# One change in five parts to a fused attention and feed-forward layer: shared score tenancies in PSUM, reversed denominator order, a first projection in halves, interleaved memory features, and an input loaded straight into the residual buffer

## The chip, the cores and the metric

The kernel runs on one core of a Trainium2 chip. Times are device microseconds of whole executions; a median is over the runs named beside it. The profile of an execution gives its span, which is 1.7 to 2.0 us shorter than its time (914.6 for 916.63). Kernels are compared only within the same rounds.

## The reference, cut to what matters

2048 tokens of width 1024, 32 heads of 32, four segments of 512 tokens. Each segment has causal attention inside itself and reads a memory `M`, `z` that the earlier segments have filled. Then come a projection, a residual and a gated feed-forward part of width 3584.

```python
h = x + _A_ref(_layernorm(x), A_wq, A_wk, A_wv, A_wo, A_beta)
h2 = h + _B_ref(_layernorm(h), B_w1, B_w3, B_w2)
# in _A_ref, for each segment s of 4:
p = _softmax(q @ k * scale + mask);  a_dot = p @ v
pq = phi(q);  a_mem = (pq @ M) / (pq @ z + 1e-6)      # phi(t) = t + 1 if t > 0, else exp(t)
outs.append(g * a_mem + (1 - g) * a_dot)
pk = phi(k);  M = M + pk @ v;  z = z + sum(pk)
```

## The kernel before

The kernel describes all its work as operations with a cost, a class (a lower number goes first) and the buffers that they read and write. Before anything runs, a scheduler plays the operations through with rough costs and fixes the order of each engine's instructions. The chip keeps that order (all 5472 weight loads of TensorE come in the same order in the changed kernel's trace and in e1's): if an operation takes longer than its estimate, what stands behind it on its engine waits (in e10 an exponential stands on ScalarE behind a feature exponential that waited 1.37 us). This is the part of it that the argument needs:

```python
# schedule(), cut: an operation on an engine is taken by class, when its inputs are ready
if o.patience and mode == "full" and now < o.offered + o.patience:
    skipped.append(item)          # a column block waits a while rather than change the array's use
    ...
if not can_start(o):              # no free PSUM bank
    skipped.append(item)
```

The kernel divides PSUM, the memory that TensorE writes into, into eight banks. A tenancy is one stay of results in banks, from the first matmul that writes them to the read that frees them. Banks 0 to 3 are for one score tenancy at a time, 4 and 5 hold the values and denominators of a head group, and 6 and 7 serve all dense work (projections, memory updates, output projection):

```python
def dense_group(self, late=False):
    g = Group([(6,), (7,)], ("att", [(4,), (5,), (0,), (1,), (2,), (3,)]) if late else None, True)
```

A head group is four heads, and its attention is a "unit". TensorE uses the array in three ways: full (128x128), rows (four scores at once on 32 rows each), and columns (four value or denominator matmuls at once on 32 columns each). In the timelines these are `128*128`, `32*128` and `128*32`, and the four of a set start within 0.012 us.

```python
def unit(self, s, g, q, k, v, pq):                     # cut
    for batch in (0, 1, 2):
        gr = self.queue(0, 1, 2, 3)
        kcs = ((0,), (1,), (2, 3))[batch]
        width = (512, 384, 384)[batch]                  # three tenancies per unit
        ...                                             # 4 or 8 score matmuls, then one exp
    for kc, src in pieces():                            # values and denominators alternate
        for g_, what in ((gn, "n"), (gd, "d")):
            ...
    # o1 = values * ocol * R0;  o2 = Nm * R1;  oT = o1 + o2

def wo_stage(self, s):                                  # cut
    for i in range(4):
        t = 4 * s + i
        xr, h, hn = self.xr[0], self.h[t % 2], self.hn[0]
        self.g.dma(xr[:, :], self.x2d[t * 128:(t + 1) * 128, :], cls=2)
        for half in range(2):
            gr = self.dense_group(s >= 2)
            ...                                         # 8 matmuls with wo
            # h = xr + PSUM on VectorE, class 3, which frees the dense bank
        self.ln(16 + t, h[:, :], hn[:, :], 4)           # statistics, then hn from h
```

The softmax here doesn't subtract the row's maximum and nothing guards it: scores larger than these inputs give would overflow.

## Time and profile before

| | before |
|---|---|
| time, median of 3 | 918.27 us (917.35 to 918.42) |
| span of the profiled execution | 914.6 us |
| streaming of all matmul columns | 874.3 us |
| changes of array use | 234, at 0.109 us: 25.5 us |
| head: waits and clock ramp up to the first projection | 6.8 us |
| waits of TensorE after it | 3.65 us |
| end: drain and store after the last matmul | 2.9 us |

How to read it: the streaming is every matmul's columns / 2.4 GHz + 2.5 ns, a set of four row-tiled or column-tiled matmuls counted once. This is the line through the spacings in the trace of before: the next matmul, or set, of the same use starts after 0.0557 us at 128 columns, 0.1092 at 256, 0.1625 at 384 and 0.2158 at 512. A change of use is counted at 0.109 us; the prediction lists the measured medians, 0.104 to 0.116. The clock ramp is in the starts of the first matmuls of 512 columns: about 0.43 us apart up to 4.2 us, 0.216 from 4.5 us on. The head is the time from TensorE's first instruction (1.24 us) to the first projection, less the streaming between. The waits are what remains between the first projection and the last matmul. The prediction shows the lines of the page, the timeline of the array's changes, and the head.

### The profile page before, as it was taken

The numbers are of one execution on the slowest core, as the hardware profiler recorded it, in microseconds if no ns is written. First come the engines' busy times: TensorE is split into PE (matmuls) and PEld (weight loads), VectorE is DVE, ScalarE is ACT, GpSimd is POOL, SyncE is SP. The second block draws the span as 40 slices with busy tenths as digits, with TensorE's granted clock in tenths as the row PEclk, the third lists the DMA queues.
The fourth block names the chain that finished last, engine by engine and source line by source line (L and its number), as shares of the span: only waits on it lengthen the run. The fifth ranks groups of instructions, "written<-read, shape, count | busy, mean of one in ns | idle before, by whom it ended". The sixth has DMA issues, their size and how long they took to land.

```text
span 914.6 us, 12864 instructions
## 1 busy us (share of the span) xinstructions
PE 895.2 (98%) x5346; PEld 402.7 (44%) x5440; DVE 431.8 (47%) x739; ACT 295.2 (32%) x330; POOL 173.5 (19%) x274
## 2 busy tenths in 40 slices
PE   7999999999999999999999999999999999999998
PEld 3444444444444444444444444444444444444443
DVE  3677857788767775644634411211343334431111
ACT  4777546886777751111111100000111111110000
POOL 3454505665554441100100000000000000000000
PEclk9999999999999999999999999999999999999999
DMA  9769774542513119543733121012133212301110
GB/s 310 196 186 220 163 203 125 152 120 94 137 47 93 47 51 319 144 131 93 205 94 93 51 65 47 21 34 83 48 98 92 67 48 70 93 24 41 35 40 29
DMA packets 145241, 96.26 MB, mean 105 GB/s; under 512 B 45344, under 2 KB 132384, under 8 KB 145184
## 3 DMA queue, kind: packets, MB, share of 16 engines
q1 hardware_dynamic: 145184, 95.45, 37.9%
q8 instruction: 43, 0.70, 0.3%
q14 instruction: 14, 0.11, 0.0%
HBM read 76.55 MB, written 8.39 MB: 93 GB/s over the span
## 4 chain that ended last, share of the span: by engine, by line
PE 95%; DVE 2%; issue 1%; ACT 1%; DMA 0%; POOL 0%; SPq 0%; ACTq 0%
PE ps L604 88%; PE ps L927 4%; PE ps L874 3%; DMA xs<-in_A_x_dram 0%; DVE lnst L725 0%; DVE h L982 0%; DVE t L1011 0%; DVE hm L1016 0%; ACT eA L889 0%; ACT sg L1008 0%; PE ps L616 0%; ACT eB L889 0%; DVE T L938 0%; ACT xnT L627 0%; DVE xs L734 0%
## 5 line engine op out<-in xcount | busy, mean ns | idle before, releaser
L604 PE MATMUL ps<-hnT,w1b 128*128 128x512 bf16 x877 | 220.6, 379 | 1.4 <-issue 0.6
L604 PE MATMUL ps<-hnT,w3b 128*128 128x512 bf16 x877 | 220.2, 379 | 1.3 <-issue 0.5
L1008 ACT ACTIVATE sg<-ps 128x512 bf16<-128x512 f32 x112 | 66.9, 597 | 427.7 <-PE ps L604 427.7
L604 PE MATMUL ps<-w2b,hm 128*128 128x512 bf16 x878 | 195.4, 379 | 0.9
L1011 DVE SCALAR_TENSOR_TENSOR t<-sg,ps 128x512 bf16<-128x512 bf16 x112 | 76.9, 687 | 195.3 <-ACT sg L1008 195.1
L604 PEld LDWEIGHTS ps<-w2b,hm 128*128 128x128 bf16 x896 | 87.6, 98 | 105.8
L604 PEld LDWEIGHTS ps<-hnT,w3b 128*128 128x128 bf16 x896 | 87.0, 98 | 104.8 <-issue 0.9
L604 PEld LDWEIGHTS ps<-hnT,w1b 128*128 128x128 bf16 x896 | 87.0, 98 | 104.4 <-issue 5.5
L1016 DVE SCALAR_TENSOR_TENSOR hm<-t,ps 128x512 bf16<-128x512 bf16 x112 | 76.9, 687 | 37.3 <-PE ps L604 34.1
L1038 DVE TENSOR_TENSOR ob<-hr,ps 128x512 bf16<-128x512 bf16 x32 | 22.0, 687 | 143.4 <-PE ps L604 143.4
L889 ACT ACTIVATE eA<-ps 128x2048 bf16<-128x2048 f32 x32 | 60.0, 1875 | 15.2 <-PE ps L874 11.1
L604 PE MATMUL ps<-xnT,wp 128*128 128x512 bf16 x246 | 59.4, 380 | 3.7 <-issue 1.3
L604 PE MATMUL ps<-hnT,wp 128*128 128x512 bf16 x248 | 59.4, 380 | 1.5 <-issue 0.8
L604 PE MATMUL ps<-wo,oT 128*128 128x512 bf16 x247 | 58.3, 379 | 1.1 <-issue 0.6
L889 ACT ACTIVATE eB<-ps 128x1536 bf16<-128x1536 f32 x32 | 46.3, 1448 | 12.7 <-PE ps L874 12.6
L889 ACT ACTIVATE eC<-ps 128x1536 bf16<-128x1536 f32 x32 | 46.4, 1450 | 10.4 <-PE ps L874 10.4
L894 POOL TENSOR_SCALAR_AFFINE_SELECT eC<-eC 128x512 bf16<-128x512 bf16 x64 | 41.2, 667 | 44.0 <-ACT eC L889 44.0
L938 DVE STREAM_TRANSPOSE T<-ps 128x512 f32<-128x512 f32 x32 | 22.9, 716 | 31.5 <-PE ps L927 31.3
L604 PEld LDWEIGHTS ps<-wo,oT 128*128 128x128 bf16 x256 | 23.9, 98 | 28.9 <-issue 2.1
L604 PEld LDWEIGHTS ps<-xnT,wp 128*128 128x128 bf16 x256 | 22.9, 98 | 30.4 <-issue 3.9
L604 PEld LDWEIGHTS ps<-hnT,wp 128*128 128x128 bf16 x256 | 23.4, 98 | 28.9 <-issue 2.6
L874 PE MATMUL ps<-qT,kT 32*128 32x256 bf16 (+3 forms) x512 | 34.5, 302 | 0.4 <-ACT eB L889 0.3
(98 smaller groups left out, 718.0 us busy)
## 6 DMA issues: line engine op xcount, KB each, us to landing
w1b<-in_B_w_dram SPq DMA_DIRECT2D x28, 512.0 KB, 3.9
w3b<-in_B_w_dram SPq DMA_DIRECT2D x28, 512.0 KB, 4.9
wp<-in_A_wk_dram SPq DMA_DIRECT2D x8, 1024.0 KB, 5.8
wp<-in_A_wv_dram SPq DMA_DIRECT2D x8, 1024.0 KB, 6.1
wp<-in_A_wq_dram SPq DMA_DIRECT2D x7, 1024.0 KB, 6.4
w2b<-in_B_w_dram SPq DMA_DIRECT2D x7, 1024.0 KB, 8.1
xs<-in_A_x_dram SPq DMA_DIRECT2D x16, 256.0 KB, 6.9
xr<-in_A_x_dram SPq DMA_DIRECT2D x16, 256.0 KB, 3.1
```

Of the source, the lines that this page charges most:

```text
L604: return [e.matmul(p[0](gr), p[1], p[2], start=p[3], stop=p[4]) for p in part]
L874: ins.append(e.matmul(self.bank(gr, j, n, off), k[r, g, 128 * kc:128 * kc + 128], q[r, g, 128 * kc:512], start=True, stop=True, tile_posit ...
L889: return [e.activation(et[:, :, :], src, AF.Exp, scale=self.scale)]
L894: self.pool_op(lambda e, m=m: e.affine_select(m, m, pattern=[[0, 4], [1, 128]], compare_op=ALU.is_ge, fill=0.0, base=0, channel_multiplier ...
L927: ins.append(e.matmul(self.ps[r, b * 512 + 128 * kc:(b + 1) * 512], lhsT, src[:, j, :], start=first, stop=True, tile_position=(0, 32 * j), ...
L938: G.op("dve", dve_ns(512), lambda e, gr: [e.transpose(T1, self.bank(gr))], writes=[T1], cls=0, group=gd)
L1008: self.g.op("act", act_ns(512), lambda e, gr, sg=sg: [e.activation(sg, self.bank(gr), AF.Tanh, scale=0.5)], writes=[sg], cls=2, group=gg)
L1011: e.scalar_tensor_tensor(t1, sg, 1.0, self.bank(gr), op0=ALU.add, op1=ALU.mult)], reads=[sg], writes=[t1], cls=2,
L1016: e.scalar_tensor_tensor(dst, t1, 0.5, self.bank(gr), op0=ALU.mult, op1=ALU.mult)], reads=[t1], writes=[dst], cls=2,
L1038: self.g.op("dve", dve_ns(512), lambda e, gr, hs=hs, ob=ob: [e.tensor_tensor(ob, hs, self.bank(gr), op=ALU.add)], reads=[hs], writes=[ob], ...
```

## The change

The intent: fewer changes of array use, a shorter start, and dense work spread more evenly through attention. Five parts, with the diff cut to its core:

```diff
 # (1) two head groups share five full tenancies (6 shared score buffers), not six of 512, 384, 384;
 #     to make room, the sums of a unit are made in place
+        ta = self.scores(s, [(a, 0, 0)])
+        tb = self.scores(s, [(a, 3, 384), (a, 1, 0)])
+        tc = self.scores(s, [(a, 2, 0), (b, 2, 256)])
+        self.finish(s, a, ...)
+        ta = self.scores(s, [(b, 0, 0)])
+        tb = self.scores(s, [(b, 3, 384), (b, 1, 0)])
+        self.finish(s, b, ...)
...
-        dst = o1 if s else oT
+        dst = R0 if s else oT
...
-            self.either(lambda e: e.tensor_tensor(o2, Nm, R1, op=ALU.mult), ...
-            self.either(lambda e: e.tensor_tensor(oT, o1, o2, op=ALU.add), ...
+            self.either(lambda e: e.tensor_tensor(Nm, Nm, R1, op=ALU.mult), ...
+            self.either(lambda e: e.tensor_tensor(oT, R0, Nm, op=ALU.add), ...
 # (2) denominators in reverse order, and column blocks may wait longer for a turn
+            order = [("n", 0), ("n", 1), ("n", 2), ("n", 3), ("d", 3), ("d", 2), ("d", 1),
+                     ("d", 0)]
-        o.patience = 2600.0
+        o.patience = 4000.0
 # (3) the first query projection by token halves
+                if n == 0:
+                    self.first_q(w)
+                    continue
 # (4) key features and memory updates interleaved (query features already were); residual and memory
 #     additions in class 1
+            if s:
+                self.phi(self.qT[s % 2][:, 2 * pr:2 * pr + 2, :], self.pq[pr % 2][:, :, :], 3)
+            if s < 3:
+                self.memory(s, pr)
+            self.pair(s, pr)
...
-                self.memory(s)
 # (5) x goes straight into the residual buffer, of which there are three; the staging buffer goes
-            xr, h, hn = self.xr[0], self.h[t % 2], self.hn[0]
-            self.g.dma(xr[:, :], self.x2d[t * 128:(t + 1) * 128, :], cls=2)
+            h, hn = self.h[t % 3], self.hn[0]
+            self.g.dma(h[:, :], self.x2d[t * 128:(t + 1) * 128, :], cls=2)
...
-                    hs, xs, self.bank(gr), op=ALU.add)], reads=[xs], writes=[hs], cls=3,
+                    hs, hs, self.bank(gr), op=ALU.add)], reads=[hs], writes=[hs], cls=1,
```

The prediction treats (4) and (5) together, as its part 4. The whole diff also puts the other projections in class 5 instead of 6, changes two of the scheduler's cost estimates (scores and column blocks) and drops an unused mask.

## The prediction

One passage is cut from the prediction; its mark stands where it was. The sum came to 918.3 - 3.05 - 1.8 + 0.1 - 0.6 = 912.95 us. The -0.6 is the author's estimate; the rest is worked out from the trace of before and the edit, and that trace has 50 matmuls of the feed-forward part starting in 10.79 us (0.2158 each) and about 0.11 us for a change of use. That the weight loads run under the matmuls is on its page: 402.7 us of loads beside 895.2 of matmuls in a span of 914.6.

> **What bounds the kernel now.** I read the page first: busy shares, the granted clock, the chain that ended last.
>
> ```profile
> PE 895.2 (98%) x5346; PEld 402.7 (44%) x5440; DVE 431.8 (47%) x739; ACT 295.2 (32%) x330; POOL 173.5 (19%) x274
> PEclk9999999999999999999999999999999999999999
> PE 95%; DVE 2%; issue 1%; ACT 1%; DMA 0%; POOL 0%; SPq 0%; ACTq 0%
> ```
>
> TensorE is busy 98% and its own instructions are 95% of the chain that ended last, at full granted clock; no other engine reaches half of the span. So a saving on VectorE, ScalarE, GpSimd or the DMA queues is worth only the TensorE wait that it removes. The sharper question is what lies between TensorE's 914.6 us and the bare streaming of its columns. For that I read the timeline of TensorE, matmul by matmul, in the attention part.
>
> ```profile
> 200.44 0.28 PE L927 MATMUL ps<-eC,v 128*32 128x256 bf16 x4
> 200.55 0.28 PE L927 MATMUL ps<-eC,ones 128*32 128x256 bf16 x4
> 200.66 0.23 PE L927 MATMUL ps<-eC,v 128*32 128x128 bf16 x4
> 200.72 0.23 PE L927 MATMUL ps<-eC,ones 128*32 128x128 bf16 x4
> 201.11 0.81 PE L604 MATMUL ps<-xnT,wp 128*128 128x512 bf16 x3 [0.16 <-issue]
> 201.85 0.40 PE L874 MATMUL ps<-qT,kT 32*128 32x512 bf16 x4
> 202.18 0.63 PE L604 MATMUL ps<-v,pkn 128*128 128x129 bf16 x8
> ```
>
> The first column is the start, and starts are what to subtract; the second is a latency that overlaps. Four row-tiled or column-tiled matmuls start within 0.01 us and share the array, so a set of four 256-column ones takes 0.11 us, of 128 columns 0.06 us. A set of 512 columns should take 0.216 us, but from the scores at 201.85 to the next full matmul 202.18 - 201.85 = 0.33 us pass: 0.11 us too many. I computed this excess at every boundary between the three uses of the array (full 128x128, row-tiled scores, column-tiled value and denominator matmuls), against columns/2.4 GHz plus 2.5 ns per matmul. The medians: full to row 0.106, row to full 0.111, row to column 0.109, full to column 0.104 us, whatever the width that stands last.
>
> Column to full looks dearer (201.11 - 200.72 = 0.39, an excess of 0.34), but it is a trap. There are 5440 weight loads and 5346 matmuls, so 94 matmul records are missing; here the timeline has three of the group's four, and two weight loads before the first recorded one (0.876 and 0.891 past 200). The missing matmul therefore started near 200.89, and the excess is 0.34 - 0.22 = 0.12 us like the others. Two such boundaries with complete records show 0.116 us.
>
> The budget of the 914.6 us then is: streaming of all 5440 matmuls 874.3; 234 changes of array use at 0.109, 25.5; start before the first real projection about 8 (clock ramp and waits, 1.2 us before the first instruction); waits inside the attention part 3.1, the longest 0.67, 0.59 and 0.50; the rest is the final drain and store. The streaming is out of the change's reach.
>
> The head comes from the timeline of the first 26 us:
>
> ```profile
> 4.73 1.67 PE L604 MATMUL ps<-oT 128*128 128x512 bf16 x7
> 9.01 1.61 PE L616 MATMUL ps<-ident,xs 128*128 128x128 bf16 x24 [2.60 <-DVE xs L734]
> 11.49 0.61 PE L616 MATMUL ps<-ident,xs 128*128 128x128 bf16 x8 [0.87 <-DVE xs L734]
> 13.30 10.60 PE L604 MATMUL ps<-xnT,wp 128*128 128x512 bf16 x47 [1.21 <-ACT xnT L627]
> ...
> 9.66 2.01 ACT L627 ACTIVATE xnT<-ps 128x1024 bf16<-128x1024 bf16 x2 [2.74 <-PE ps L616]
> 10.19 0.69 DVE L628 COPY xnT<-ps 128x1024 bf16<-128x1024 bf16 x1
> 12.13 1.02 ACT L627 ACTIVATE xnT<-ps 128x1024 bf16<-128x1024 bf16 x1 [0.46 <-PE ps L616]
> ```
>
> The first projection waits for all four token tiles; the last is copied out of PSUM only at 12.13 + 1.02 = 13.15, though tiles 0 and 1 are there at about 10.7 and 10.9.
>
> [...] the largest gap here is 2.6 us and the granted clock stays full, so shortening the head buys only its own time.
>
> **The change part by part.**
>
> 1. Scores in full tenancies. Before, a head group has three PSUM tenancies of 512, 384 and 384 columns, 96 in all; after, two groups share five of 512, 80 in all. Columns are the same (2 x 1280 = 5 x 512), so streaming is not reduced. What goes is visits: 16 fewer row-tiled blocks. With the scheduler's reordering, the built program's TensorE order has 235 blocks of like use before (107 full, 96 row, 32 column) and 207 after (95, 80, 32): 28 changes fewer. 28 x 0.109 = 3.05 us, all on the path since TensorE is it. On ScalarE, 2048-element exponentials take 1.875 us and 1536-element ones 1.449, so a fixed part of about 0.17 us (estimate by the line through both): 64 x 1.449 + 32 x 1.875 = 152.7 becomes 80 x 1.875 = 150.0. These 2.7 us are beside the path.
>
> 2. Reverse order of the denominator. It puts the 512-column set last in 24 of 32 column blocks. If the apparent 0.34 us were real this would save 23 x 0.23 = 5.3 us. By the missing record above it isn't, so I book 0. Equal weights follow each other, but each is loaded again and the loads already run under the matmuls.
>
> 3. First query by token halves. By the new order: tiles 0 to 2 transposed, then the first 8 half matmuls, tile 3 transposed, then the rest. Start at about 11.0 (copies done at 10.9; the second half of the weights lands at 10.3); 8 x 0.109 = 0.87 to 11.87; eight transposes at 0.056 to 12.32, copied out by about 13.5; 24 x 0.109 = 2.62 to 14.94, past that copy, so no wait; 32 x 0.109 = 3.49 to 18.4. Before: 13.30 + 32 x 0.216 = 20.2. Gain 1.8 us. The split adds 32 matmuls, 32 x 2.5 ns = 0.08 us.
>
> 4. Interleaved query and key features, memory updates and residual additions at a higher class, x loaded straight into a triple-buffered h. These touch the 3.1 us of waits only:
>
> ```profile
> 219.51 1.04 PE L604 MATMUL ps<-xnT,wp 128*128 128x512 bf16 x4 [0.49 <-DVE h L982]
> 241.32 1.04 PE L604 MATMUL ps<-xnT,wp 128*128 128x512 bf16 x4 [0.18 <-DVE h L982]
> 52.28 1.04 PE L604 MATMUL ps<-xnT,wp 128*128 128x512 bf16 x4 [0.33 <-DVE kT L628]
> 78.23 1.02 PE L604 MATMUL ps<-hnT,wp 128*128 128x512 bf16 x4 [0.42 <-DVE qT L628]
> ```
>
> The first two (excess 0.67 and 0.34) are residual additions late in VectorE's queue, which the higher class can cure. The others come from a short 8 x 0.056 = 0.45 us memory group between two dense groups with two banks, shorter than the 0.69 us copy that must free a bank; the new order still has such places. New waits will appear too. I book -0.6 of 3.1.
>
> Sum: 918.3 - 3.05 - 1.8 + 0.1 - 0.6 = 912.95, say 913.0 us, 0.6% faster.
>
> **The rivals.** (a) The apparent column-to-full cost is real: then 5.3 us more go, about 908. For: 30 of those boundaries show 0.34. Against: the extra weight load, and the complete records at 0.116. (b) A new wait takes the place of the visits. In-place R0 and Nm now stay occupied until the final addition, and the shared score buffer lives through both groups of a pair; column blocks wait up to 4.0 us for a turn rather than 2.6. For: all order is fixed at build time from rough costs. Against: a unit lasts some 10 us (320 us for 32), much over these chains of about 1 us each, and dense work stands between. If the waits double, 916 to 917. (c) The head gains nothing, as the next key projection then waits for its weights or for query evictions: weights land at 13.3, well before 18.4, and four evictions at 0.60 run while the last half streams. At worst 914.8. (d) ScalarE becomes the bound: it has 62.9 of 87 us busy from 24 to 111 and loses work, so no.
>
> **Range and chances.** The counts (28 changes) are certain and their price stable to 5%; the head is good to 0.7 us; the waits can move from -2 to +3. Executions spread about 1 us. That gives 910.0 to 916.0. Over 2% faster means under 899.9: without any wait, streaming 874.4, 206 changes 22.5, a head of 6.2, an end of 3.2 and the 3.6 us by which the timed median exceeds the profiled span still make 910, so 1%. Over 2% slower needs 18 us of new waits, six times those of before: 1%.
>
> **What would show it.** Right: 206 changes with the same 0.11 us each; weight loads and matmuls up by 32; first projection at about 11.0 and its end near 18.4; 80 exponentials of about 1.875 us; column to full with 512 last no cheaper than 0.11 to 0.12 us. Wrong: waits in the attention part that sum to more than 4 us, above all of memory groups or score tenancies, or a first key group that starts later than 19.

## More of the kernel before

One more line belongs here, for later. It is a row of the list of instruction groups, ScalarE, of the kernel before:

```profile
L889 ACT ACTIVATE eA<-ps 128x2048 bf16<-128x2048 f32 x32 | 60.0, 1875 | 15.2 <-PE ps L874 11.1 <-PE ps L927 3.8
```

After the bar stand busy time and nanoseconds of one, then ScalarE's idle time just before them and what ended it. The exponential mostly waits for its own scores (11.1 us), and for 3.8 us its wait ends with a column block, which reads the exponentials' buffers.

## The result, and the profile after

The changed kernel took 917.41 us (median of 4, 916.1 to 918.23), the kernel before beside it 918.35 (median of 4, 917.35 to 919.37). The ratio is 0.9988, 95% interval 0.9971 to 1.0006. A ratio here is the mean time of one kernel's fast runs over that of the other's of the same rounds, so it is not quite the ratio of the medians. The time lay 4.4 us above the predicted 913.0 and above the range. Of the 5 us of gain less than 1 was left.

The page of the changed kernel, with the lines that answer to those of the prediction:

```profile
PE 904.0 (99%) x5472; PEld 404.1 (44%) x5472; DVE 432.8 (47%) x735; ACT 297.7 (32%) x316; POOL 176.2 (19%) x274
PEclk9999998999999999999999999999999999999999
PE 96%; ACT 1%; DVE 1%; DMA 0%; issue 0%; SPq 0%; DVEq 0%
```

TensorE is the bound as before. The row of granted clock has an 8 in its seventh slice, where there were only nines. The weight loads and matmuls are both 5472, so no record is missing in this profile.

| budget, profiled execution | before | changed | difference |
|---|---|---|---|
| changes of array use x 0.109 us | 234: 25.5 | 206: 22.45 | -3.05 |
| head | 6.82 | 4.71 | -2.11 |
| waits after it, half clock included | 3.65 | 10.30 | +6.65 |
| span | 914.6 | 916.2 | +1.6 |

The three differences add up to +1.5, which is the span's +1.6 but for 0.1 of streaming. The parts that save did save, and the waits took it back. Next is TensorE's timeline at the start of the changed kernel:

```profile
10.74 1.03 PE L598 MATMUL ps<-xnT,wp 128*128 128x256 bf16 x8 [0.26 <-DVE xnT L622]
11.61 0.61 PE L610 MATMUL ps<-ident,xs 128*128 128x128 bf16 x8
12.06 9.73 PE L598 MATMUL ps<-xnT,wp 128*128 128x256 bf16 x72
21.72 0.40 PE L871 MATMUL ps<-qT,kT 32*128 32x512 bf16 x4
```

The first eight half matmuls start at 10.74 (before 13.30), the fourth tile is transposed right behind them, and the 72 that follow run without a wait. 56 of them are query halves, so the first query ends at 12.06 + 56 x 0.109 = 18.16; the prediction had 11.0 and 18.4.

The disputed change from column to full can be read at the end of a column block, in the changed kernel and in a second profile of the same program (run e1), which has lost 95 of its matmul records:

```profile
89.59 0.23 PE L939 MATMUL ps<-et,ones 128*32 128x128 bf16 x4
89.75 1.90 PE L598 MATMUL ps<-wp,hnT 128*128 128x512 bf16 x8
```

```profile
PE 895.4 (98%) x5377; PEld 404.2 (44%) x5472; DVE 432.7 (47%) x735; ACT 297.7 (32%) x316; POOL 176.1 (19%) x274
...
89.94 0.23 PE L939 MATMUL ps<-et,ones 128*32 128x128 bf16 x4
90.32 1.67 PE L598 MATMUL ps<-wp,hnT 128*128 128x512 bf16 x7 [0.16 <-issue]
```

With all records the next full matmul starts 0.16 us later. With one lost, 7 are listed instead of 8, the gap looks like 0.38 us, and an "issue" wait of 0.16 us appears that does not exist. Over all 30 such boundaries the excess, with the 0.01 us by which the first matmul after a change is longer, is 0.116 us in the complete profile, for 128 columns last (7 cases) and for 512 last (23); in the incomplete one its median is 0.342 for both.

Where did the waits come from? The list of TensorE's waits, first of the kernel before (two of its rows, which the change touches), then of the changed one. The columns are total, times and longest, in us:

```profile
PE ps L604 <- DVE h L982: 0.7, 2, 0.5
PE ps L874 <- ACT eB L889: 0.3, 1, 0.3
```

```profile
PE ps L871 <- ACT et L884: 2.0, 5, 0.8
PE ps L598 <- DVE R0b L970: 1.5, 1, 1.5
PE ps L598 <- DVE h L993: 0.9, 3, 0.6
```

Scores wait for exponentials, and single groups wait for VectorE. Most of it stands in one place, around 150 us. This is the changed kernel's timeline there, cut to what matters:

```profile
144.59 0.83 DVE L725 TENSOR_SCALAR hn<-h,lnmv,rstd 128x1024 bf16<-128x1024 bf16 x1
145.45 1.24 SPq L210 DMA_TRANSPOSE hnT<-hn  x1
146.24 0.71 PE L939 MATMUL ps<-et,ones 128*32 128x128 bf16 x16
146.74 0.58 SPq L203 DMA_DIRECT2D h<-in_A_x_dram  x1
146.89 1.04 PE L598 MATMUL ps<-wo,oT 128*128 128x512 bf16 x4
147.01 1.88 ACT L884 ACTIVATE et<-ps 128x2048 bf16<-128x2048 f32 x1 [1.99 <-PE ps L939]
147.79 0.39 PE L598 MATMUL ps<-pq,zsel 128*128 128x512 bf16 x1
148.94 0.40 PE L871 MATMUL ps<-qT,kT 32*128 32x256 bf16 x8 [0.77 <-ACT et L884]
150.05 0.71 DVE L970 SCALAR_TENSOR_TENSOR R0b<-ps,ocol,R0b 128x512 f32<-128x512 f32 x1
150.68 1.08 DVE L725 TENSOR_SCALAR hn<-h,lnmv,rstd 128x1024 bf16<-128x1024 bf16 x1
150.81 0.52 PE L598 MATMUL ps<-pq,Mbf 128*128 128x512 bf16 x1 [1.47 <-DVE R0b L970]
151.32 0.61 PE L871 MATMUL ps<-qT,kT 32*128 32x512 bf16 x4
151.68 1.27 DVE L993 TENSOR_TENSOR h<-h,ps 128x512 bf16<-128x512 bf16 x2
152.50 1.86 PE L598 MATMUL ps<-hnT,wp 128*128 128x512 bf16 x4 [0.56 <-DVE h L993]
```

Between the last output projection at 146.89 and the next dense group at 152.50 TensorE has no dense work. By the kernel's assignment of banks the two dense ones hold the two finished halves of that projection until the residual additions at 151.68 read them. These additions need x in their residual buffer. Its load was only issued at 146.74: the buffer was read by the layer normalisation of the tile three before until 145.42 (144.59 + 0.83), and a transpose stands ahead of the load in the queue until 146.69. It landed at 150.79, when VectorE had just begun the next normalisation, 150.68 to 151.76. Meanwhile only attention work is left, and it runs bare into its own chains: scores for an exponential of 1.88 us, the memory matmul for VectorE to empty its bank. The waits here are 0.83 + 1.52 + 0.19 + 0.62 = 3.2 us against the pure pitch.

Then the clock falls. The view by stretches of the changed kernel, whose last three columns are granted clock, DMA share and GB/s:

```profile
140.00:147.50 7.50, 7.35 (x72) 3.07 (x69) 6.32 (x13) 4.82 (x4) 5.30 (x8) 1.00 0.55 79
147.50:151.00 3.50, 1.26 (x12) 0.31 (x10) 3.43 (x8) 3.00 (x2) 2.01 (x3) 0.99 0.71 183
151.00:158.00 7.00, 6.44 (x25) 2.58 (x24) 4.10 (x8) 1.55 (x3) 5.30 (x9) 0.52 0.58 132
```

TensorE is busy 1.26 of 3.5 us, and for the next 7 us the granted clock is 0.52: exactly, half clock from 150.95 for 6.83 us, which costs 3.0 us. Other runs show single stretches of 3.41 us (e4, e8, e10). The waits in the hole are no longer than 1.5 us, while at 8.71 us in this same profile TensorE had waited 2.42 us at full clock, and the clock stayed full.

The recorded stretches of full and half clock all begin on a grid of 3.413 us, whose place differs from execution to execution (first mark at 4.17 us in this profile, 4.41 in e1, 6.37 in e4). A window is here the stretch between two marks. The last one before the fall was this:

```profile
147.53:150.94 3.41, 1.17 (x12) 0.31 (x10) 3.34 (x8) 2.91 (x2) 1.95 (x3) 1.00 0.70 182
```

Streaming, by the formula of the budget, fills 0.23 of it. The profiles have six falls inside a program, and the window just before holds 0.23 (here and in e1), 0.24 (e6), 0.27 (e8), 0.29 (e4) and 0.31 (e10). No other window at full clock, in the 17 profiles that record the clock, that ends before the last matmul holds less than 0.36. So in these profiles the fall goes with what is streamed in one window, and not with the longest wait; what makes it is not shown. The same head fell in one profile and not in another: its lowest window holds 0.39 in the profile of the kernel before, at full clock, and 0.29 in that of e4, whose grid lies elsewhere, before the fall.

The fall is not certain. Six executions of the changed kernel in e1 have a mean granted clock of 1.0 (915.72 us), 0.998 (916.21 and 916.63) and 0.996 (917.6 to 918.23). The kernel before has such stretches too: beside e1 to e4 its executions at 1.0 took 916.15 to 917.7, those at 0.998 took 917.9 to 919.1.

So without the half clock the waits are where the prediction's rival b put them: doubled, from 3.65 to about 7.3 us. Why they doubled is what the experiments are for.

### The profile page after: what moved, and what is told of

Same layout as the page of the kernel before. It is cut to its first block, busy times and chain, and to the rows that moved or that the text cites. A ratio compares the mean times of both kernels' runs of the same rounds, so it can differ in the third digit from the quotient of the medians.

```text
span 916.2 us, 12998 instructions
## 1 busy us (share of the span) xinstructions
PE 904.0 (99%) x5472; PEld 404.1 (44%) x5472; DVE 432.8 (47%) x735; ACT 297.7 (32%) x316; POOL 176.2 (19%) x274
## 4 chain that ended last, share of the span: by engine, by line
PE 96%; ACT 1%; DVE 1%; DMA 0%; issue 0%; SPq 0%; DVEq 0%
PE ps L598 89%; PE ps L939 4%; PE ps L871 3%; ACT et L884 1%; DMA xs<-in_A_x_dram 0%; DVE lnst L716 0%; PE ps L610 0%; DVE h L993 0%; DVE hn L725 0%; SPq L203 0%; DVE T L950 0%; DVE R0b L965 0%; DVE R0b L970 0%; DVE qT L622 0%; DVE xnT L622 0%
## 5 line engine op out<-in xcount | busy, mean ns | idle before, releaser
L598 PE MATMUL ps<-hnT,w1b 128*128 128x512 bf16 x896 | 223.2, 379 | 0.0
L884 ACT ACTIVATE et<-ps 128x2048 bf16<-128x2048 f32 x80 | 149.9, 1874 | 34.2 <-PE ps L871 17.9
L889 POOL TENSOR_SCALAR_AFFINE_SELECT et<-et 128x512 bf16<-128x512 bf16 x128 | 88.7, 710 | 118.6 <-ACT et L884 118.3
L598 PE MATMUL ps<-hnT,wp 128*128 128x512 bf16 x256 | 63.5, 390 | 0.9 <-DVE h L993 0.6
L598 PE MATMUL ps<-xnT,wp 128*128 128x512 bf16 (+1 forms) x288 | 60.2, 356 | 0.3 <-DVE xnT L622 0.3
L598 PEld LDWEIGHTS ps<-xnT,wp 128*128 128x128 bf16 x288 | 26.5, 98 | 27.1 <-issue 4.2
L976 POOL TENSOR_TENSOR Nm<-Nm,R1b 128x512 f32<-128x512 f32 x24 | 30.4, 1268 | 32.6 <-DVE R1b L965 32.5
L871 PE MATMUL ps<-qT,kT 32*128 32x128 bf16 (+3 forms) x512 | 31.9, 302 | 2.2 <-ACT et L884 2.0
L598 PE MATMUL ps<-wp,hnT 128*128 128x512 bf16 x128 | 30.8, 380 | 0.0
```

The costliest lines, as they stand in the source:

```text
L598: return [e.matmul(p[0](gr), p[1], p[2], start=p[3], stop=p[4]) for p in part]
L871: ins.append(e.matmul(self.bank(gr, j, 512 - 128 * kc, off), k[r, g, 128 * kc:128 * kc + 128], q[r, g, 128 * kc:512], start=True, stop=Tru ...
L884: return [e.activation(et[:, :, :], src, AF.Exp, scale=self.scale)]
L889: self.pool_op(lambda e, m=m: e.affine_select(m, m, pattern=[[0, 4], [1, 128]], compare_op=ALU.is_ge, fill=0.0, base=0, channel_multiplier ...
L976: self.either(lambda e: e.tensor_tensor(Nm, Nm, R1, op=ALU.mult), 512, 2, [Nm, R1], [Nm], 2)
```

## The experiments

Theory at the start: part (5) makes the hole, because x arrives late in a buffer that is still in use. Rivals: the shared tenancies and buffers do it by themselves; the in-place sums do it; the order of the denominators or the head gives nothing. All runs gave correct results. All differ from the kernel before by less than 2%. Ratios are against the kernel before of the same rounds, times are medians. Both include executions with and without half clock. "Waits" are those of the budget after the first projection, half clock included. Runs of the kernel before: 916.95 us for e1 to e4, 917.42 for e5 to e8, 918.11 for e9 to e12, and 917.46 for e13 to e16.

**e1: the changed kernel again.** No edit.

> The changed kernel once more, as the yardstick of this chip. Late-x theory and its rivals alike: 917.4 us give or take 1, TensorE waits of about 7 us after the first projection, 3.0 of them between 147 and 153 us, and a stretch of half clock of about 3.4 or 6.8 us right after it (in how many windows the clock falls may differ from execution to execution).

917.11 us (915.72 to 918.23), ratio 0.9998 [0.9985, 1.0010]. Waits 10.2, with half clock from 151.2 for 6.83 us. The hole is in the order, not an accident of one execution.

**e2: four residual buffers.** Layer normalisation's statistics are kept in rings of 6 to make the room; the rings alone leave the instruction order as it is.

```diff
-        self.h = [buf(f"h{i}", [128, 1024], BF16) for i in range(3)]
+        self.h = [buf(f"h{i}", [128, 1024], BF16) for i in range(4)]
-            h, hn = self.h[t % 3], self.hn[0]
+            h, hn = self.h[t % 4], self.hn[0]
```

> The changed kernel with a ring of four buffers for x and h instead of three (the room comes from normalisation statistics kept in rings of six, which alone leaves the instruction order as it is). Late-x theory: tile 3's x no longer waits for tile 0's normalisation, the hole near 150 us and the half clock go, about 3.0 + 3.0 us: 912 us (210 changes of array use against 206 cost 0.4 of it). Rival, in-place R0 and Nm hold bank 4: these are untouched, the hole and the half clock stay, 917. Rival, shared score tenancies starve TensorE: untouched too, 917.

912.58 us (912.34 to 912.98), ratio 0.9949 [0.9936, 0.9962]. Waits 4.4 with 210 changes of use, no half clock. One more buffer gives 4.5 us against e1.

**e3: x in a staging buffer of its own again, and two residual buffers.** All other parts as changed.

```diff
+        self.xr = [buf(f"xr{i}", [128, 1024], BF16) for i in range(1)]
-        self.h = [buf(f"h{i}", [128, 1024], BF16) for i in range(3)]
+        self.h = [buf(f"h{i}", [128, 1024], BF16) for i in range(2)]
-            self.g.dma(h[:, :], self.x2d[t * 128:(t + 1) * 128, :], cls=2)
+            self.g.dma(xr[:, :], self.x2d[t * 128:(t + 1) * 128, :], cls=2)
```

> The changed kernel with x staged in its own buffer as before and h in two; everything else as changed. Late-x theory: no hole near 150 us, clock full throughout, about 911.5 us (207 changes of array use). Both rivals: hole and half clock stay, 917.

911.90 us (911.44 to 913.33), ratio 0.9943 [0.9932, 0.9955]. Its list of TensorE's waits:

```profile
PE ps L872 <- ACT et L885: 1.3, 2, 0.8
PE ps L599 <- DVE t L1024: 1.0, 2, 0.8
```

Waits 4.0 in all with 207 changes, no half clock; the hole is gone. 0.0057 x 917 = 5.2 us, about what the prediction booked for its parts 1 and 3 (3.05 + 1.8). The shared tenancies, in-place sums and shared score buffers are all still in, so they don't need to cost anything.

**e4: the reversed denominators alone, on the kernel before.**

```diff
+        order = [("n", 0), ("n", 1), ("n", 2), ("n", 3), ("d", 3), ("d", 2), ("d", 1),
+                 ("d", 0)] if s else [(w, kc) for kc in range(4) for w in "nd"]
```

> The kernel before with only the denominator matmuls in reverse order after the first segment; instruction order and changes of array use otherwise the same, 234. Missing-record theory: nothing to gain, 918.3 within 0.5 of the kernel before, column to full about 0.116 us with 512 columns last as with 128. Rival, column to full really costs 0.34 us after a 128-column set: 22 such boundaries now end with 512 columns, 22 x 0.23 = 5 us less, 913.

917.64 us (916.27 to 918.99), ratio 1.0004 [0.9992, 1.0017]: nothing, as booked. Rival a would have made it 5 us faster. Its profile also had a half clock stretch of 3.41 us, at 13.2 us, in a head that the change of this run does not touch.

**e5: the first query by token halves alone, on the kernel before.**

```diff
+                if n == 0:
+                    self.first_q(w)
+                    continue
```

> The kernel before with only the first query projection by token halves. Head theory: first projection at 10.4 to 11.1 us in place of 13.3, the head 2 us shorter and nothing given back, as TensorE has work from then on: about 2 us under the kernel before of these rounds, 915. Rival, given back: the next weights or later waits take it again, within 0.5 us of the kernel before.

914.71 us (914.5 to 916.17), ratio 0.9974 [0.9961, 0.9988], so 2.4 us. Part of this is the clock: four of the nine executions of the kernel before were under 1.0, and one of these five. Between the medians of those at 1.0 (914.7 and 916.55) it is 1.9 us. The first projection starts at 11.54 rather than 13.30, later than the 10.4 to 11.1 expected, so the head is 1.3 us shorter in this profile and not 2; the changes are the same 234 and the waits 3.9. Rival c falls.

**e6: the changed kernel with two residual buffers instead of three.** If the late x is the cause, this must be worse.

```diff
-        self.h = [buf(f"h{i}", [128, 1024], BF16) for i in range(3)]
+        self.h = [buf(f"h{i}", [128, 1024], BF16) for i in range(2)]
```

> The changed kernel with a ring of two buffers for x and h in place of three (a dose: two, three, four). Late-x theory: x of every tile waits for the normalisation of the tile before last, so the hole of the first residual stage stays or grows (3 us or more of waits between 140 and 160 us, half clock after it) and the second stage, near 235 us, gets one as well: 919 to 924 us. Rival (the ring has nothing to do with it, the gain of the ring of four was a lucky order): no more than 1 us from the changed kernel, no second hole.

921.44 us (921.18 to 922.87), ratio 1.0047 [1.0034, 1.0060]. Waits 13.7. VectorE's list of waits names the load itself, and a second hole opens in the next segment, in this timeline:

```profile
DVE h L993 <- DMA h<-in_A_x_dram: 3.3, 4, 1.1
```

```profile
231.33 0.58 SPq L203 DMA_DIRECT2D h<-in_A_x_dram  x1
233.05 0.40 PE L871 MATMUL ps<-qT,kT 32*128 32x512 bf16 x4 [1.98 <-ACT et L884]
234.34 1.27 DVE L993 TENSOR_TENSOR h<-h,ps 128x512 bf16<-128x512 bf16 x2
234.61 0.73 PE L939 MATMUL ps<-et,v 128*32 128x512 bf16 x16 [0.84 <-ACT Nm L921]
```

The four additions of that row, which waited 3.3 us for x, stand at 376 to 453 us, where no hole is. At the second hole the load was issued at 231.33 and landed at 234.14, and the additions began at 234.34. TensorE waits 2 us at 233 for an exponential, at a time when they have not yet freed the dense banks. The dose works in both directions: two buffers 921.4, three 917.1, four 912.6.

**e7: the shared tenancies alone.** From e3, every other part is undone; the in-place sums stay, for room, and so do the two new cost estimates.

```diff
-                if n == 0:
-                    self.first_q(w)
-                    continue
-        if s:                              # reversed denominators
-            order = [("n", 0), ...
+        if True:
-        o.patience = 4000.0
+        o.patience = 2600.0
-            if s < 3:
-                self.memory(s, pr)
+                for pr in range(4):        # ahead of attention(s)
+                    self.memory(s, pr)
```

> Shared full score tenancies alone: the changed kernel with x staged as before, first query whole, denominators in the old order, memory features ahead of the attention, old classes and patience (the sums in place stay, for room). 208 changes of array use against 234: 26 x 0.109 = 2.8 us less than the kernel before if the waits in the attention part stay at 3.1 us: 914.3. Rival, tenancies shared by two groups make TensorE wait for exponentials: waits of 6 us or more and no gain, 917.

917.88 us (917.64 to 917.99), ratio 1.0005 [0.9992, 1.0017]. 208 changes, so 2.83 us saved, but waits of 7.8, and no gain is left. The rival came true. TensorE waits mostly for exponentials here:

```profile
PE ps L867 <- ACT et L880: 3.0, 8, 0.8
PE ps L932 <- ACT Nm L917: 1.3, 2, 0.7
```

So the part with the surest saving gives nothing by itself, with no late x at all. This is the first result that the theory does not cover.

**e8: e3 with the memory features and updates ahead of attention, as before.**

```diff
-            if s < 3:
-                self.memory(s, pr)
+                for pr in range(4):        # ahead of attention(s)
+                    self.memory(s, pr)
```

> Changed kernel, x staged as before (911.9 us), and in addition memory features of all pairs queued ahead of the attention as before instead of interleaved. If interleaving matters only through TensorE waits: about the same 206 changes and head, waits up by 1 to 4 us: 913 to 916. If it is worth nothing: 912.

915.67 us (914.02 to 915.77), ratio 0.9976 [0.9964, 0.9989]. Against e3 interleaving is worth about 3 us by the ratios. Waits are 8.1, of which one half clock stretch of 3.41 us makes about 1.7. So one half of the prediction's part 4 is a real gain here, and the other half more than ate it. That it works by spreading dense work between the score tenancies is likely, but not shown.

**e9: x loaded straight into one of three residual buffers, alone, on the kernel before.**

```diff
-        self.h = [buf(f"h{i}", [128, 1024], BF16) for i in range(2)]
+        self.h = [buf(f"h{i}", [128, 1024], BF16) for i in range(3)]
-            self.g.dma(xr[:, :], self.x2d[t * 128:(t + 1) * 128, :], cls=2)
+            self.g.dma(h[:, :], self.x2d[t * 128:(t + 1) * 128, :], cls=2)
```

> The kernel before with one part of part 4 alone: x is loaded straight into a residual buffer, of which there are three, and the staging buffer is gone. Theory (the late load of x into a buffer that layer normalisation still holds makes the new waits, whatever the rest of the change): waits above the 3.7 us of before, by 1 to 4 us, with a residual addition released late by a load; 918 to 921. Rival (the hole needs the denser schedule of the changed kernel, in which tenancies and memory updates leave no dense work to fill it): waits within 1 us of before, 916 to 918.

917.19 us (917.03 to 917.53), ratio 0.9991 [0.9978, 1.0004]; waits 4.95 with 231 changes. The waits are up by 1.3 us, the low end of the theory's range, but no addition waits for a load, and the ratio shows no loss. The simple form of the theory falls: the move of x does not cost 5 us wherever it is made. It cost that in the changed kernel's order, and about 1 us of waits at most in that of before. Nor does a late x always cost: in the kernel before one addition waits 2.1 us for x, at 116 us, and TensorE has no hole there.

**e10: the in-place sums alone, on the kernel before** (rival b's first clause).

```diff
-        dst = o1 if s else oT
+        dst = R0 if s else oT
-            e.tensor_tensor(o2, Nm, R1, op=ALU.mult)
-            e.tensor_tensor(oT, o1, o2, op=ALU.add)
+            e.tensor_tensor(Nm, Nm, R1, op=ALU.mult)
+            e.tensor_tensor(oT, R0, Nm, op=ALU.add)
```

> The kernel before with one thing alone: the sums of a unit are made in place (R0 and Nm stay occupied until the last addition), rival b of the prediction. Theory: a unit lasts 10 us and these chains 1 us, so nothing: within 0.7 us of before. Rival b: the occupied buffers delay the next unit; waits up by 2 us or more, 919 or over.

922.53 us (920.3 to 925.02), ratio 1.0050 [1.0033, 1.0068]. A surprise, and the time that rival b expected: waits of 10.4 (a half clock stretch of 3.41 us included). But the timeline at the longest of them does not show the chain that rival b had in mind:

```profile
222.32 1.61 DVE L801 TENSOR_TENSOR pq<-phe,phr 128x1024 bf16<-128x1024 bf16 x1 [0.47 <-PE ps L604]
...
223.97 1.06 ACT L579 ACTIVATE phe<-qT 128x1024 bf16<-128x1024 bf16 x1 [1.37 <-DVE pq L801]
...
224.93 1.43 ACT L889 ACTIVATE eC<-ps 128x1536 bf16<-128x1536 f32 x1
226.26 0.68 ACT L912 ACTIVATE Nm<-ps,gcol 128x512 f32<-128x512 f32 x1
...
226.42 0.40 PE L874 MATMUL ps<-qT,kT 32*128 32x512 bf16 x4 [2.02 <-ACT eC L889]
```

The scores at 226.42 wait 2 us for an exponential that stands on ScalarE behind a feature exponential, which waited for VectorE's feature sum. Nm is copied after that; no occupied Nm is in the chain. The feature sum took 1.61 us, where undisturbed ones in this run take 0.69; GpSimd's addition `oT<-R0b,Nm` ran beside it. The kernel before has such a pair too (1.58 us at 205.4), so this again is a matter of where the order puts them. What the in-place sums changed is the order that the build made: 230 changes of array use rather than 234, and in the exponentials' row

```profile
L889 ACT ACTIVATE eA<-ps 128x2048 bf16<-128x2048 f32 x32 | 60.0, 1874 | 20.9 <-PE ps L927 17.9 <-PE ps L874 2.7
```

17.9 us that end with column blocks, where there were 3.8. In e3, a fast version, such waits are 19.2, so they alone do not tell what TensorE loses.

**e11: e3 without the first query by halves.** A test of whether parts add up.

> The version with x staged apart (911.9) without the first query by token halves; the head is then that of before, start near 13.3. If parts add up: 911.9 + 2.1 = 914.0, between 913.4 and 915. Rival (the gain of the head is taken back by what follows): below 913.

914.12 us (913.28 to 915.5), ratio 0.9959 [0.9945, 0.9973]. The first projection starts at 13.22, waits are 4.1: the sum of the parts, 914.0, is met.

**e12: e3 with less patience of the column blocks.**

```diff
-        o.patience = 4000.0
+        o.patience = 1500.0
```

> The version with x staged apart (911.9) where column blocks may wait 1.5 us for a turn rather than 4.0. Changes of use 208 against 207. Theory (what is left to gain is waits, of which a shorter patience leaves fewer): waits 2 to 3.5 us instead of 4.0, 910.5 to 911.7. Rival (patience moves waits about and doesn't lessen them): 911.5 to 913.5.

911.03 us (910.72 to 914.03), ratio 0.9929 [0.9912, 0.9946]. Waits 3.2 with 208 changes. This is the best version found by its median, 0.7% faster than the kernel before; its interval overlaps that of e3.

**e13: the changed kernel with the product in R1 instead of Nm.** Nm comes free one addition earlier. The changed kernel's copies into Nm waited 4.9 us for such additions on VectorE and 4.3 on GpSimd.

```diff
-            e.tensor_tensor(Nm, Nm, R1, op=ALU.mult)
-            e.tensor_tensor(oT, R0, Nm, op=ALU.add)
+            e.tensor_tensor(R1, Nm, R1, op=ALU.mult)
+            e.tensor_tensor(oT, R0, R1, op=ALU.add)
```

> The changed kernel with one thing undone: the product of Nm and R1 goes into R1 rather than in place into Nm, so that Nm comes free one addition earlier. 201 changes of use instead of 206, worth 0.5 us. If the late load of x alone makes the hole: it stays, waits with half clock 9 to 11, 916 to 917.5. If the occupation of Nm shares the guilt: waits with half clock under 7, under 914. ScalarE's waits of Nm's copy for the addition (9.2 us in the changed kernel) should be gone in either case.

914.25 us (913.93 to 915.92), ratio 0.9969 [0.9957, 0.9982]. The number lies between both answers, and the profile explains why. The waits without half clock are 7.0, as in the changed kernel; what is gone is the half clock (five executions, four at a clock of 1.0) and 5 changes of use. ScalarE's waits of Nm's copy for the addition fell from 9.2 to 2.6. The hole is still there, at the same place in its timeline, and now the addition waits for x visibly:

```profile
147.21 0.58 SPq L203 DMA_DIRECT2D h<-in_A_x_dram  x1
...
149.38 0.40 PE L871 MATMUL ps<-qT,kT 32*128 32x512 bf16 x4 [1.01 <-ACT et L884]
...
150.41 1.28 DVE L993 TENSOR_TENSOR h<-h,ps 128x512 bf16<-128x512 bf16 x2 [0.80 <-DMA h<-in_A_x_dram]
...
150.93 0.73 PE L939 MATMUL ps<-et,v 128*32 128x512 bf16 x16 [0.84 <-ACT Nm L921]
```

The clock does not fall here. In this execution the grid has a mark at 149.49, between the two waits, and the windows on both sides are filled with streaming to 0.59 and 0.57:

```profile
146.08:149.49 3.41, 2.40 (x21) 0.78 (x19) 3.41 (x7) 1.88 (x2) 2.33 (x4) 1.00 0.63 128
149.49:152.91 3.42, 2.42 (x40) 1.17 (x38) 2.62 (x6) 1.34 (x2) 2.44 (x3) 1.00 1.05 225
```

**e14: the kernel before with R0 in place and the product in R1.** The edit is e10's first line with e13's last two. TensorE's order is exactly that of before.

> The kernel before with its sums in R0 and in R1 rather than in Nm (no o1, no o2); TensorE's order is exactly that of before. If Nm's occupation made the 4.4 us of the in-place version: as before, 917 to 918.7. If R0's did: 920 or over.

917.75 us (916.47 to 918.19), ratio 1.0001 [0.9989, 1.0014], waits 3.8. The occupation of R0 costs nothing where the order is the same. By the test it is the product in Nm that makes e10's loss, and with it comes e10's other order.

**e15: e2 (four residual buffers) with the product in R1.**

> The changed kernel with four residual buffers (912.6) and the product in R1. If both occupations cost by themselves and add up: 911 to 912. If only the order that the build makes counts: anywhere within 911 to 915. 202 changes of use against 210 are worth 0.9 us.

915.43 us (914.76 to 915.65), ratio 0.9977 [0.9963, 0.9990], 202 changes, waits 8.0. Two cures together are 2.6 us worse than one by the ratios. Two of its three longest waits (1.07 us, at 150.1 and 227.6) are scores behind an exponential with a single piece of four dense matmuls (0.86 us) to cover 1.88 us; around 150 us the residual additions do not wait for x. So the late x is not needed for waits of 8 us.

**e16: e12 with the product in R1.**

> The best version so far (x apart, patience 1.5 us, 911.0) with the product in R1: 205 changes of use against 208 (0.3 us), and 7.6 us of ScalarE's waits for Nm gone, which are mostly beside the path: 910 to 911.2. Rival: its waits were the order's and grow again by 1 us or more, 911.5 to 913.

912.31 us (911.97 to 914.27), ratio 0.9948 [0.9936, 0.9961], 205 changes, waits 4.4. The rival was right: freeing Nm helps nothing here, and the new order waits 1.2 us more.

**What the sixteen say together.** The waits after the first projection, half clock included, in us:

| x loaded | memory updates | waits in each profile |
|---|---|---|
| apart, order of before | ahead | before 3.65, R0 in place (e14) 3.8 |
| apart, tenancies of before, other edits | ahead | e5 3.9, e4 5.3 (half clock in it), in-place sums (e10) 10.4 (half clock in it) |
| apart, shared tenancies | interleaved | e3 4.0, e11 4.1, e12 3.2, e16 4.4 |
| apart, shared tenancies | ahead | e7 7.8, e8 8.1 (half clock in it) |
| straight into h, shared tenancies | interleaved | changed 10.3, e1 10.2, two buffers 13.7, product in R1 7.0, four buffers 4.4, four with R1 8.0 |
| straight into h, tenancies of before | ahead | e9 4.95 |

Two things are shown. In the changed kernel's setting (shared tenancies, interleaved), x in a buffer of its own gives waits of 3.2 to 4.4 us in four programs out of four, and x in the residual buffer gives 7.0 to 13.7 in four out of five (e1 is the changed kernel again), worse with fewer buffers. And each edit, even one that frees a buffer, gives another order, whose waits differ by several us for reasons in no single buffer (e7, e10, e15). What stays open: why exactly the scheduler's order in e10 is worse than that of before, and what in the orders of e7 and e15 makes their waits.

## Why the prediction was wrong

- Part 1, 28 changes at 0.109 us, -3.05: right in count and price, 206 and -3.05. What it took for granted was that a change saved is time saved. In e7 the 26 fewer changes came with 4.2 us more waits; in e3, with the other parts, the saving stood. ScalarE's exponentials are 149.9 us, as worked out, and beside the path, so rival d falls.
- Part 2, booked 0: right (e4, ratio 1.0004), and the reason too, though of the 30 boundaries said to show 0.34 two do not, those with complete records: the complete profile shows 0.116 us, the incomplete one of the same program 0.342.
- Part 3, -1.8: right in mechanism, a little small. The head is 2.1 us shorter in the changed kernel. Alone the part gives 2.4 us by the ratio and 1.9 at full clock, with a head 1.3 us shorter in its profile (e5).
- Part 4, "I book -0.6 of 3.1" (3.65 by the budget of this document): this is the step that failed. The waits of the whole change measured +6.65 us: about 3.2 in one hole of the order, 3.0 of half clock that followed it, and the rest spread. Against e3, which differs by the move of x alone, they are +6.3. The prediction took the waits of before as the stock from which something is removed, and saw in the move of x only a removed buffer. It did not follow the new place of the load: it is issued only when layer normalisation lets go of the buffer that it needs, queued behind a transpose, and lands 4 us after issue; until then two dense banks are held. Interleaving, in the same part, was worth about 3 us beside the shared tenancies (e8 against e3), where the whole part was booked at 0.6.
- Rival b came near the number (waits doubled, 916 to 917), in part by luck: the 917.4 hold 3.0 us of half clock, which it did not have. It named in-place sums, shared score buffers and patience. R0 in place costs nothing (e14). The product in Nm costs 4.5 us on the kernel before, with another order (e10 against e14); in the changed kernel undoing it left the waits without half clock as they were (e13), and in the best version it did not help (e16); the shared buffers are all in e3, whose waits are 4.0. Patience is worth 1.3 us between e3 and e12 by the ratios, within their intervals, and 0.8 by the waits. The late x was in no rival. It appears only in the list of what would show the prediction wrong, as waits of over 4 us, and there memory groups and score tenancies were suspected; the score tenancies were where the waits showed.
- The clock was set aside, as "shortening the head buys only its own time". The kernel before already lost time by it in some of its executions, and e4's profile has the fall in the head itself. This is the likely reason that the median of before exceeds the profiled span by 3.6 us where 1.7 to 2.0 is the usual difference; the prediction carried these 3.6 us over as a constant. And in the changed kernel 3.0 us of half clock followed the new hole.
- The range (waits from -2 to +3) was too narrow for a program whose whole order is rebuilt by each edit. Sixteen orders show waits between 3.2 and 13.7.

## What to carry to other kernels

When the order of instructions is fixed at build time, a saving on the bounding engine is only worth what the new order's waits leave of it: predict those as a wide range, and build two or three neighbours of a change (another buffer, another patience) before judging it. For every buffer that a change merges with another, follow the load into it: what must let go of it first, what stands ahead in the queue, when it lands, and which banks are held until then. Where the clock falls, add up what is streamed in each window of its grid: in these profiles that told a fall (0.23 to 0.31 before the six falls, 0.36 or more in every other window at full clock before the last matmul), and the longest wait did not. And before a boundary is called dear, check in the counts of weight loads and matmuls that no record is missing: here 0.116 us read as 0.342.
